# A recurrence taken by 1,024 tokens instead of 512, with its inputs in borrowed space, three spectrum buffers instead of four, and a new written order

## The chip, the core and the metric

The kernel runs on one core of a Trainium2 chip. A core has a matrix engine (TensorE, PE in the profile; PEld is its loading of weights), VectorE (DVE), ScalarE (ACT), GpSimd (POOL) and SyncE (SP), which here issues all transfers. SBUF is the working memory of 128 partitions; PSUM, in eight banks of 512 fp32 columns per partition, takes what TensorE computes; VectorE and ScalarE read it out. The metric is the device time of one execution in microseconds.

## The reference

A gated recurrence over 6,272 tokens feeds a long convolution with two multiplicative gates. Four batches, 256 channels, all fp32.

```python
sig = 1.0 / (1.0 + np.exp(-f_logit))
f = lower_bound + (1.0 - lower_bound) * sig
for t in range(S):
    h = f[:, t] * h + (1.0 - f[:, t]) * x[:, t]
    y[:, t] = h
proj = y @ w_proj                       # 256 -> 768: x1, x2, x3
X2 = np.fft.rfft(x2, n=S, axis=1)
H = np.fft.rfft(filter_fft, n=S, axis=0)
x2_conv = np.fft.irfft(X2 * H, n=S, axis=1)
out = (x1 * x2_conv * x3) @ w_out
```

## The kernel before

*Recurrence, `hgrn(b)`, lines 322 to 384.* The 6,272 tokens of a batch are 12 pieces of 512 and one of 128. For each piece two transfers bring the logits and x (L334), ScalarE applies the sigmoid of the negated logit (L337), GpSimd multiplies it into x (L339), and for each half of the channels (`kh`) TensorE transposes both (the step `su`, L351) into two PSUM banks, logits and products in the halves of each; ScalarE or VectorE makes the factor f from the transposed sigmoid (step `f`, L364 and L366), and VectorE runs the scan (L372), which starts from the last column of the scan before it and writes h to `HA`. The first 3,072 tokens are also copied behind the end (step `wrap`, L380), so that circular reads need no wrap. Inputs lie in three pairs of buffers (`XT`, `FL`), in batch 0 also in `gx`.

*Spectrum.* The convolution is a Fourier transform of length 49 x 128 in two factors. Step `P` (L725) projects h to x2, gathered by residues of 49, and its eviction writes `X2`, one row of `PW` = 116 half-words per channel pair, with gaps at columns 49 to 63 and 113 to 115 that hold zeros. `F1` (L737) and `F2` (L795) are the two transform factors, for 16 units of 8 channel pairs; F1 is evicted into one of four slots of `A`. The product with the filter's spectrum (L816 on VectorE straight out of PSUM, or an eviction by ScalarE and L825 on GpSimd) reads a buffer of `Hu`, 512 KB, loaded from DRAM (L772) for each unit; batches go through the units up and down in turn, so that the last buffers' units are still there for the next batch. `I2` (L835) and its eviction `Th` lead back. Four products per batch for the lone frequency columns (`mini`, `zm` at L761) read `Hm`, which lies in the gaps of `X2`.

*Gates and output.* `x13` (L400) projects h to x1 and x3, whose product is `zt` (evictions at L291, L293, L296, L298; products at L422 on VectorE or L431 on GpSimd, through `gx`). Step `I1` (L869) finishes the inverse transform, `y` (L875) multiplies it with `zt`, `proj` (L887) applies w_out, and an eviction and a store (L911) write the rows out.

*Preparation.* The filter's spectrum is computed on the core first (L637, L661, L679) and stored to DRAM; `afs` are the two buffers between its two factors, one of them the fourth spectrum buffer `Hx`.

*The order.* Nothing is scheduled by the compiler. Each step is recorded with what it reads and writes and with a cost per engine; the string `ORDER` then lists all steps in three characters each: number, engine and PSUM bank. Each engine, SP's queue of transfers too, takes its steps in that order, and semaphores follow from the reads and writes. The recurrence of batch b + 1 stands inside the spectrum and output steps of batch b; the first P of a batch needs all scans of it. `prod` marked MUL is L816, otherwise an eviction and a `pm` (L825).

Of the kernel before, what the change touches and what calls it, by code (L numbers as in the profile page):

```python
# [32 lines left out]
NH = 4  # L33
# [31 lines left out]
class Plan:  # L65
# [63 lines left out]
    "AAYA+gBBgAMYABIAZVACIBFgAaSBMgAtRBPgAmXAqSBTgAdTBIgA9YANIAcSBagAbUAoQAvVAwXA/WBCABDQBAGBGSBEIBogAOABdgBQAAPIBNQBWg"  # L129
    "BhgBHCBkgDwgBUVBOADxgBJYD8gBRTBVFEIgAuRArQBKQBSLBbWD9gBLABeYASIAQAATYADgAxTBXIAVYBcGAsVAyRBfTAUIEJgBYQBgDBpYBiWARI"  # L130
    "EUgBZABlIAWYBqSBmUBjGBrKApTBnMAhQAgQAfXAeTEVgAkRBuQDyABwSB1UBxKBvAB3WB2MBzSByYB4GDzYB+QD+AB0KCAWB6UCBGB/IEKAD0SB7M"
    "B5YAEYD4QD1CCFWD/YEggD5ICHUAFgD2KCGGEhgCIECDWCKUD6ICEGEASCCYELYCLEEBKEEWAlRECKEtgEFGCOQEsgCXUCPACJYAXYEGOCVSEWAEMQ"
    "CYMEiAEQWEXYCQUE4gEROCWCB8gAIACRME5gAKAESOCTSENABsYEYUCUCEOIEcWFCgCeSEdGCSYCZYEZMFDgCgQEjYAHAEeOCfCChACaSEaMEuACnQ"
    "EkWCbCEvYCoIClUElOE6AEoQCjSEmOFNgCmEFMgCkCCiYAjUCpYEpIEwUEnYAJAE7YCwWEqIExEETgE0SCxGEyMFWgCqQE1CCNgC1WCrAFXgE2KE8U"
    "FEAE/QC2OC3SFggFAAFFYE9MCuWFhgC4CAGgFBICvGAiTCMgFOACzWE+MFGSCyYC0GFPYFJQFHKC+UFqgFKAFIKFrgC6WC/EB9gC7GFQUAYYFLIDAS"
    "FYADHWFRMFTQDBCC5YFZYFSMDIGF1gDFSFUACsgDQWF0gDGCDDUFVID7gFiADKSDCYEzYEfgDEMFaQDRGEPYDLCDXWDJYCtgFbIErYDVUALADOSFjY"
    "DYODWEFcIDPCFdWDNgFsADTUD3gFeOFkQDUEMTgDSYFtYFfODgSFlAFnUEbgDhCFmICcgDeWFoEAnSDaSDZYF2AFpMDfGFuQF3YDbCDlWE3YFvIDnU"
    "EDYDmGDdgF+gDjSFwIDiYDoEEHgBtYFxWCdgDkCDpYJQVMfgFyODqQDcgJSFFzOC8gJRTDrAJVVMUgJWSC9gJTrJXFF4WF7QJYCJUYDuUF8IF5GF9I"
    "F/gDsgJZYJaTDvEF6ODtgJbQGAWDMgJdIMVAJcLGQUGigGBOJeYGGQGRMGUSGHAG0gGSWGVCMggGCUGTGGIRG9gGDEGEWGJJMhAGMUGFGGKRGNMGrg"
    "GOWGLJGWTGPGJfRGXDJgWJkQJiOJlXJhBJmIGeSJjYGYVGfCJnvJpUJqQJoYGZFJrMGaSJuRJsIGbCGjWJwJJtYGcUGnuJvQGdEJzSJ0RJxoGoYJ1C"  # L140
    "J4XGluJyYJ2BGsUGgSG1QJ3YGwEGhKGmYHQgJ5WJ6PG5AMrgHGSGtYMsgGkYJ9VJ7uGxYHHCJ+RGusJ8YGpWJ/FHMSGqGG3oGvYG+UG6YHZgKABHIW"
    "HNKG4YGyQHJGHAsHKSGzAG2YHigKBYG7WHLCHCsHBYKCQG/YG8GHORHRTHDYHrgHPJKDVHTDHVrHSYKHXKEAHUYKITKJHKFtKMSHWYMtAHEQKKrKGY"
    "KOKHaWKLYHFAMuYH+gH0UHcuHXSH1EH4QHeuHdYHYCHjUHbYHkYH5AHlsHfYIHgH2WMWYHgSH3GHnsHmYHsQHhCH6WHuoHoYIQgHpUHtYH7GMiYH/S"
    "HwoHvYHqEH8WKNQIBCIIUH9OHxYIZgIDqIRRICYIKEHyWITBKPoIEYKRUHzGIMsKQYKSTIiQIAYKTEIsgILYIFWIjAINYKUrKWVKVYKXTIGGKYNMXQ"
    "KZDIJYIVpI1gISYIaWIUYMYAMbUIeGMZIIWYIOSM3gMcEM4gKbXIPCMdMKaYI+gIXQKdHImSIYAIcuIbYMegMjUIfYInCIkQMkMIdYIoWIlAKcTMlM"
    "KgSMaYJHgIpGItQKerKiCIqUMnWIvoKfYIxAKhTNDgMoGIyYIgRIrMNEgIwYM5AMpOKlQI2UIhBKjrMvWIuYKnAI3YI6sKkYMzSM6YMwGKmQNPgI4E"
    "MxOKqRI7YNQgM0CIzUKsBM1KM7WI5YI0ENFAKrVKooKvTKttKpYM8GM/QNGYKuYKxDJIUM9ONbgNAAI8SNcgJMENBIKwXJKEK0WI9CJLYI/UKyvK2G"
    "K1RJBsKzYNHSK3BNRAK5WJDsJCYJAYK4YNLQNICNlgK7OJEYJFUNMANSYNmgNJKK6WJGEK+XNdANNINKgK/VNTTLAHJJYNeYK8uNXQNUDLBtK9YLDX"
    "NvgNYANVLLEWLCYMygLFHLISNwgLJVLKCNOgLNXJNYLGuLLFNfSNZILHYLPHNiUNgCLOWN6gNnANhKLMYN5gJOQNWgNjENoYLQuRtSJPANkMRuXLRY"
    "RvCLSQRwHLXSLTINxANpUMmYNsWLYKNqENyYLUQODgNtGOEgNrMLZSLVANuOLcULaCLWgNzQLdMRyWN0ALhSR0GN1IN2UN7ALmWONgN3ELiKOOgLeQ"  # L150
    "N8YLbgOFAM+gN4MLjSMqgLfALnOLrULkCOGYN9QLsMOAWN+ALoSOXgOBGN/IOYgM2gOHULpCNagOCOLwQOPAOKSLxILtWUwgOLCOQYLlgOIEOMKLyQ"
    "LuGOJML1SLzAORWL2KL0gRzROSGLqgL6UOZANCAOTOOUSOaYR1BU8gL7MU9gObWL3QOcGOVCOdOOWKOeUL4AL8WVJgVIgOfMUxgMEQL9GOgMLvgL/S"
    "MFIL5gOxUUyALggMAKOvQOyEL+gOhWOwIU+AOtUOiGO3QOuEOnWO4AOjTOoGO1ROkLUzYOpWO2BOrUOqGOzSU/YOsEOlQO0KVKAMBUOmAVLYMJWMCE"
    "O5SMKOO9QO6CMDgMGUO+IMOSMHEPDWMPKO7QPFuRxYR3SMIgO8AO/UPHuR4TR2YPGYPAEMLQR5KPtgR6DPBUPLWMMAPCMPbSPNuPEYPIYPTUR7YPdC"
    "R8QPXEPPuPOYPJRR+APMYPlVPKBPYYPVsPQYP2gR9QSBXMNgPmFPRRR/oPWYSDHPjVSAYPfqPSBPcYP/gSCQPUYPeYSGXPkFSHUSEoPgYPnSSIPSFY"
    "SJEPpQPoCPZWSKYQIgPqIPuUPaGPhSPysPrQP3WPiCPsIPzYSLVPwsP5GP4YQRQPvYSNFP6YQJSQSAP7uPxYQbgQAVSMUQEFSQRQNKP8YP0WSOsSSB"
    "QkgSRTSPYP1GQCtQBYSVQQFYSWUSXAQTWSTrQDYP9QSYsQUGSUYSaVSZYQLqQtgQOYQVTScFQGWP+AQWLQMYSbSQHGQcQQKYQ2gSdCQXUQgoQPWSeY"
    "QYESfTQeoQhYQQGQZRQlUShDQaJQfYRJgQ3WQnsQpEQmYQ/QQdYQ5GQiSQqYQ7GRAIQoYQuUQjCU0WQysQwERBQQvYU1GRSgQxYU4SQzYRCAU2OQrU"
    "VUgVVgU5CVAQQsEQ6YU6KRbgQ0WVBARDUQ1GU7gSgTVCISkSREEQ8YRKWSirSlRSmCRMuSjYSpQSnBRFUSrASqTSoYROuRNYRGESuSVEQSsrQ4YRPY"
    "SwCRHVVggSvXRINVFAStYVhgRTTRLYSxHVGIQ9VVWASyYSzSRVLS0XVHgQ+FVMQVXYRkgRXrS1CRQVVNAS2vRYYS4TRRFS5UVOIS3YS9XS6DRWYRcV"  # L160
    "S/HS7sVQSReFRgtS8YVYQVsgVRCVtgS+XRUYVZARfYVSKRhYTCWViARZUTAvVTgTDTRaETHSVaITBYVjYTIXTEGVcUTJCTFrRlQV4gVdETKvTGYTMW"
    "V5gRpARnoTNTTLYRmYTOGRdYTRXRqYTSSTTHTPrRoYVkQVuAVeMTQYRiWVlAVvYTWTTUqRjGTXUVmITVYTbVTYDVoWTdFTcRWCgVpOTZEWDgVwSV6A"
    "TaYVqORrUVxCTgQV7YTepRsEV0WVyKTfYTiAThRWMgV1GTlUVfgTmVTjpVrgTnEMQSU3YV2OToFTkYWNgTqUMRCTrRTpYTsETvSTtpV8UTuYTwKT0Q"
    "V9EV/WWEAT1IWWgTxSWXgWAGWFYVPgV+MT2QTyCWBOTzgT5UT3AMSgWGSVnYWOAT6MT+WWJQWHCWPYT/OT7UWggWKAT4gWhgWIKUAWT8EVzYWLIWQU"
# [32 lines left out]
def kernel(  # L197
# [780 lines left out]
```

## Time and profile before

| | us |
|---|---|
| median of 3 runs (460.45 to 461.36) | 460.54 |
| the profiled execution | 459.27 |
| its span, first to last instruction | 457.5 |
| TensorE busy | 443.7 |
| VectorE busy | 408.9 |
| ScalarE busy | 399.3 |
| GpSimd busy | 300.9 |

The granted clock of TensorE was 0.998 of full speed. "Busy" is a union in time; a group's "busy" is the sum of its instructions, which can overlap a little. Rows of groups read: line, engine, operation, output<-inputs, shapes, count | busy us, mean ns of one | idle us of the engine before them and what ended it. A row of a stage gives its length and then, for PE, PEld, DVE, ACT and POOL, busy us (instructions), the granted clock, the share of the 16 DMA engines and GB/s.

### The profile page before, as it was taken

The numbers are of one execution on the slowest core, as the hardware profiler recorded it, in microseconds if no ns is written. First come the engines' busy times: TensorE is split into PE (matmuls) and PEld (weight loads), VectorE is DVE, ScalarE is ACT, GpSimd is POOL, SyncE is SP. The second block draws the span as 40 slices with busy tenths as digits, with TensorE's granted clock in tenths as the row PEclk, the third lists the DMA queues.
The fourth block names the chain that finished last, engine by engine and source line by source line (L and its number), as shares of the span: only waits on it lengthen the run. The fifth ranks groups of instructions, "written<-read, shape, count | busy, mean of one in ns | idle before, by whom it ended". The sixth has DMA issues, their size and how long they took to land.

```text
span 457.5 us, 14613 instructions
## 1 busy us (share of the span) xinstructions
PE 443.7 (97%) x6009; PEld 346.2 (76%) x6009; DVE 408.9 (89%) x461; ACT 399.3 (87%) x550; POOL 300.9 (66%) x274
## 2 busy tenths in 40 slices
PE   8998999999999999999999999999999999999995
PEld 6876777767766889777668889767768897677784
DVE  7599996799999993999999986999999977999873
ACT  5989998889999989989998979999989868988563
POOL 4489892289899425778996616989896405976400
PEclk9999999999999999999999999999999999999999
DMA  8999999776979997477779995487969930575176
GB/s 323 407 366 333 357 356 347 284 262 203 313 259 298 326 339 299 179 250 246 241 272 287 350 315 240 142 288 297 308 205 308 351 124 18 192 238 179 48 294 271
DMA packets 46451, 122.59 MB, mean 268 GB/s; under 512 B 4528, under 2 KB 9648, under 8 KB 46384
## 3 DMA queue, kind: packets, MB, share of 16 engines
q1 hardware_dynamic: 46384, 121.65, 75.4%
q8 instruction: 47, 0.77, 0.7%
q14 instruction: 20, 0.16, 0.1%
HBM read 86.12 MB, written 31.98 MB: 258 GB/s over the span
## 4 chain that ended last, share of the span: by engine, by line
PE 70%; DVE 15%; ACT 8%; issue 4%; POOL 2%; DVEq 0%; ACTq 0%; POOLq 0%
PE PS L400 15%; PE PS L725 9%; PE PS L835 8%; PE PS L887 8%; PE PS L351 7%; DVE HA L372 6%; PE PS L737 6%; PE PS L795 6%; DVE ys L875 4%; PE PS L637 3%; PE PS L869 3%; PE PS L661 3%; ACT fTs L364 2%; ACT HA L291 2%; PE PS L603 2%
## 5 line engine op out<-in xcount | busy, mean ns | idle before, releaser
L339 POOL TENSOR_TENSOR XT<-XT,FL 128x1024 f32<-128x1024 f32 (+1 forms) x49 | 110.0, 2247 | 52.1 <-ACT FL L337 28.9
L372 DVE TENSOR_TENSOR_SCAN HA<-fTs,HA,PS 128x512 f16<-128x512 f32 (+1 forms) x96 | 113.2, 1203 | 1.1 <-ACT fTs L364 0.2
L400 PE MATMUL PS<-HA,W 128*128 128x490 f16 (+1 forms) x416 | 102.7, 367 | 1.0 <-DVE HA L372 0.4
L825 POOL TENSOR_TENSOR PP<-HA,Hu 98x1008 f16<-98x1008 f16 x38 | 79.7, 2104 | 5.1 <-ACT HA L291 2.7
L291 ACT CAST HA<-PS 128x1024 f16<-128x1024 f32 (+1 forms) x96 | 78.2, 837 | 5.3 <-PE PS L737 2.9
L431 POOL TENSOR_TENSOR zt<-gx 128x490 f16<-128x490 f32 (+1 forms) x43 | 52.1, 1217 | 45.0 <-DVE ys L875 16.7
L816 DVE TENSOR_TENSOR PP<-PS,Hu 98x1008 f16<-98x1008 f32 x58 | 68.1, 1200 | 0.0
L875 DVE TENSOR_TENSOR ys<-PS,zt 128x1024 fp32r<-128x1024 f32 (+1 forms) x52 | 58.9, 1152 | 7.8 <-PE PS L869 4.7
L887 PE MATMUL PS<-Wo,ys 128*128 128x256 f32 x392 | 58.2, 294 | 1.6 <-DVE ys L875 1.5
L364 ACT ACTIVATE fTs<-PS,cc 128x512 f32<-128x512 f32 (+1 forms) x83 | 54.8, 675 | 5.1 <-PE PS L351 4.3
L400 PEld LDWEIGHTS <-W 128*128 128x128 f16 x416 | 34.6, 97 | 30.4 <-issue 6.8
L835 PEld LDWEIGHTS <-PP 98*128 98x128 f16 x1024 | 49.9, 97 | 9.7 <-issue 1.6
L835 PE MATMUL PS<-VV,PP 98*128 98x98 f16 x1024 | 55.9, 206 | 0.3
L887 PEld LDWEIGHTS PS<-Wo,ys 128*128 128x128 f32 x392 | 49.7, 188 | 6.6 <-DVE ys L875 2.9
L291 ACT CAST Th<-PS 128x784 f16<-128x784 f32 x59 | 48.3, 821 | 6.6 <-PE PS L835 4.6
L293 ACT ACTIVATE gx<-PS 128x490 f32<-128x490 f32 (+1 forms) x84 | 48.3, 584 | 2.5 <-PE PS L400 1.5
L337 ACT ACTIVATE FL<-FL 128x1024 f32<-128x1024 f32 (+1 forms) x49 | 49.4, 1010 | 0.0
L725 PE MATMUL PS<-W,HA 128*128 128x256 f16 x392 | 44.6, 273 | 0.2
L351 PEld LDWEIGHTS PS<-iden,FL 64*128 64x128 f32 x736 | 31.2, 138 | 16.8 <-DVE HA L372 2.9
L725 PEld LDWEIGHTS <-HA 128*128 128x128 f16 x392 | 42.9, 142 | 1.3 <-DVE HA L372 0.3
L351 PE MATMUL PS<-iden,FL 64*128 64x64 f32 x736 | 42.2, 231 | 1.6 <-DVE HA L372 0.8
L291 ACT CAST X<-PS 128x1024 f16<-128x1024 f32 (+1 forms) x31 | 32.6, 1092 | 10.3 <-PE PS L725 9.0
(130 smaller groups left out, 745.6 us busy)
## 6 DMA issues: line engine op xcount, KB each, us to landing
FL<-in_f_logit_dram SPq DMA_DIRECT2D x45, 512.0 KB, 5.5
XT<-in_x_dram SPq DMA_DIRECT2D x45, 512.0 KB, 6.4
Hu<-H SPq DMA_DIRECT2D x39, 512.0 KB, 4.8
out_dram<-osb SPq DMA_DIRECT2D x22, 512.0 KB, 4.6
out_dram<-PP SPq DMA_DIRECT2D x16, 512.0 KB, 5.3
Hx<-H SPq DMA_DIRECT2D x13, 512.0 KB, 4.4
out_dram<-HA SPq DMA_DIRECT2D x10, 512.0 KB, 5.5
X<-in_moe_filter_fft_dram SPq DMA_DIRECT2D x9, 512.0 KB, 7.2
```

The lines of the kernel that those rows point to most:

```text
L291: nc.scalar.copy(dst, src)
L339: op("u", {"POOL": 0.1 + 0.553 * nb}, lambda e, xt=xt, ft=ft: nc.gpsimd.tensor_tensor(xt, xt, ft, op=AOP.mult), r=[("ft", k)], w=[("xt", k)])
L351: nc.tensor.transpose(bank(pb)[:, at[p] + j:at[p] + hn:nb], src[ps, j, cols], iden[ps, ps])
L364: nc.scalar.activation(fT, sT, AF.Identity, scale=by, bias=1.0)
L372: nc.vector.tensor_tensor_scan(h, fT, bank(pb)[:, 512 - hn:512 + hn], init, op0=AOP.mult, op1=AOP.add),
L400: nc.tensor.matmul(PS[:, p, 0:n], W13[:, kh, js], HA[:, HB[kh] + t0:HB[kh] + t0 + n], start=(kh == 0), stop=(kh == 1))
L725: nc.tensor.matmul(pp[:, r - r0, :], column(HB[kh], q_of(r)), W2[:, kh, :], start=(kh == 0), stop=(kh == 1))
L816: nc.vector.tensor_tensor(pr, px.unsqueeze(1).broadcast_to([TB, 2, UE, 63]), hh, op=AOP.mult)
L825: nc.gpsimd.tensor_tensor(pr, spec[:, o, :, 1:64].unsqueeze(1).broadcast_to([TB, 2, UE, 63]), hh, op=AOP.mult)
L835: nc.tensor.matmul(PS[:, ib + o, pr * TB:(pr + 1) * TB], PP[:TB, k, o, n, 2 * pr:2 * pr + 2, :], v[:TB], start=(n == 0), stop=(n == 1))
L875: nc.vector.tensor_tensor(late["ys"][:, yk, :, 0:rn * 128], PS[:, cb:cb + 2, 0:rn * 128], late["zt"][:].rearrange("p k r m -> p k (r m)") ...
L887: nc.tensor.matmul(po[:, i, :], late["ys"][:, yk, kh, i * 128:(i + 1) * 128], Wo[:, kh, :], start=(kh == 0), stop=(kh == 1))
```

## The change

From batch 1 on the recurrence takes six pieces of 1,024 tokens and the last of 128. A piece's transfers stay at 512 KB (two for the logits, two for x, each half of a partition's 8 rows), and so do sigmoid and multiplication. Logits and products are now transposed in steps of their own, each into two whole banks, with every eighth column written by one transpose; a gate and a scan take 1,024 columns. Batch 0 keeps pieces of 512 (function `single`), with the same buffers as before.

Inputs of one piece fill `XF` (which is `XT` and `FL` together); two further pieces land in `X2` (blocks of 2,048 half-words) and in what is left of `XF`; the second gate buffer `FT1` is block 6 of `X2`. So those loads wait until F1 of the batch before has read the block, and after the last scan the gaps of X2 are set to zero again (step `pad`, function `blank`). `Hm` therefore leaves the gaps for a tile of its own, in which the channel pair is the innermost index. There are three spectrum buffers, and `Hx` is gone: `afs` has two own tiles. `ORDER` is new throughout.

```diff
-NH = 4
+NH = 3
-    Hm = xv[:, :, Q:Q + 8].rearrange("m i (e a k) -> m e a k i", e=2, a=2)
-    Hu = konst.tile([128, NH - 1, 2, 2, UE * 64], F16, name="Hu")
-    Hx = konst.tile([128, 2, UE, 64], F32R, name="Hx")
+    Hu = konst.tile([128, NH, 2, 2, UE * 64], F16, name="Hu")
...
+    def load(b, t0, rows, dst, src, t):
+        n = 128 * rows
+        for j in range(0, rows, 4):
+            nj = min(4, rows - j)
+            op("load", {"SP": 0.46}, lambda e, j=j, nj=nj: nc.sync.dma_start(
+                dst(j // 4)[:, 0:nj], src[b, t0:t0 + n, :].rearrange("(p j) d -> p j d", p=128)[:, j:j + nj]),
+               w=[t[j // 4]], dma=0.38 * nj, lag=2.4, margin=MARGIN)
...
+    def scan(t0, n, kh, fT, tags, u, hn, src):
+        t1 = HB[kh] + t0
+        init = 0.0 if t0 == 0 else HA[:, t1 - 1:t1]
+        op("scan", {"DVE": 0.12 + 2.08 * n / 1000.0}, lambda e, pb: nc.vector.tensor_tensor_scan(
+            HA[:, t1:t1 + n], fT, u(pb), init, op0=AOP.mult, op1=AOP.add),
+           r=tags + ([("hn", kh, hn[0] - 1)] if t0 else []), w=[("hn", kh, i) for i in hn], src=src)
...
+    FT0 = fTs[:].rearrange("p a t -> p (a t)"), [("fT", 0), ("fT", 1)]
+    FT1 = X2[:, 2048 * 6:2048 * 7].bitcast(F32), [("xb", 6)]
...
+        slots = [(xf(0, 1), xf(2, 3)), (xb(0, 1), xb(2, 3)), (xb(4, 5), xf(4, 5))]
+        if b % 2 == 0:
+            slots = [slots[0], slots[2], slots[1]]
+        for p in range(S // 1024):
+            (ft, tf), (xt, tx) = slots[p % 3]
+            t0, nb = 1024 * p, 8
+            gate_in(b, t0, nb, ft, xt, tf, tx)
             for kh in range(2):
                 cols = slice(kh * 128, kh * 128 + 128)
+                def turn(e, pb, src, cols=cols):
+                    for j in range(nb):
+                        for q in range(2):
+                            ps = slice(64 * q, 64 * q + 64)
+                            nc.tensor.transpose(PS[:, pb + q, j::nb], src(j // 4)[ps, j % 4, cols], iden[ps, ps])
+                fT, tag = (FT0, FT1)[kh]
+                sf = op("su", {"PE": 0.5}, lambda e, pb, turn=turn, ft=ft: turn(e, pb, ft),
+                        r=tf + ["iden"], w=["qT"], take=2)
+                op("f", {"ACT": 0.145 + 1024 / 1200.0, "DVE": 0.11 + 1024 / 960.0},
+                   lambda e, pb, fT=fT, kh=kh: gate_f(e, fT, bank(pb), kh),
+                   r=["om"], w=tag, src=sf)
+                sv = op("su", {"PE": 0.5}, lambda e, pb, turn=turn, xt=xt: turn(e, pb, xt),
+                        r=tx + ["iden"], w=["qU"], take=2)
+                scan(t0, 1024, kh, fT, tag, bank, [2 * p, 2 * p + 1], sv)
+        (ft, tf), (xt, tx) = xf(0), xf(2)
+        single(b, NCHK - 1, ft, xt, tf, tx, [], [FT0, FT1])
+        op("pad", {"POOL": 2.0}, blank, w=[("xb", i) for i in range(7)] + ["pads"])
+
+    def blank(e):
+        nc.gpsimd.memset(xv[:, :, Q:64], 0.0)
+        nc.gpsimd.memset(xv[:, :, 113:PW], 0.0)
...
-        afs = [tmp.tile([128, 2, UE, 64], F32R, name="afs"),
-               Hx]
+        afs = [tmp.tile([128, 2, UE, 64], F32R, name=f"afs{i}") for i in range(2)]
...
-        f1 = op("F1", {"PE": 0.056 * UE}, mm, r=[("x2", g) for g in range(NX2)] + ["D1"], take=2)
+        f1 = op("F1", {"PE": 0.056 * UE}, mm, r=[("x2", g) for g in range(NX2)] + ["D1", "pads"] + [("xb", i) for i in range(
+            u * UE * PW // 2048, min(6, ((u * UE + UE - 1) * PW + 127) // 2048) + 1)], take=2)
...
-            nc.vector.tensor_tensor(zp[:TB, q % 2], px, Hm[:TB, :, :, :, es], op=AOP.mult)
+            nc.vector.tensor_tensor(zp[:TB, q % 2], px, late["Hm"][:TB, :, :, :, es], op=AOP.mult)
...
+            late["Hm"] = cv.tile([128, 2, 2, 2, NEP], F16, name="Hm")
```

More of the change, by code (lines that the diff above doesn't have):

```diff
@@ L651, in tails @@
             nc.gpsimd.memset(X2[:, NEP * PW:], 0.0)
-        op("pad", {"POOL": 0.6}, tails, w=[("raw", i) for i in range(7)] + [("x2", 1)])
+        op("pad", {"POOL": 0.6}, tails, w=[("raw", i) for i in range(7)] + [("x2", 1), "pads"])
         mX = tmp.tile([128, 2, NEP], F32R, name="mX")
@@ L772, in spectrum_load @@
         op("H", {"SP": 0.46}, lambda e: nc.sync.dma_start(
[L773 removed]
+            Hu[:, h][:HP].rearrange("p a e k -> p a (e k)"), turned(H[u // 2][u % 2])),
            r=[("H", u, i) for i in range(2)],
[L775 to L776 removed]
+           w=[("Hu", h)] + ([("hs", h, a) for a in range(2)] if first else []),
            dma=1.5, lag=2.0, margin=MARGIN)
```

274 lines of the change are left out of this document (135 added, 139 removed).

## The prediction

> **What bounds the kernel now.** I read the page first, then the busy time by stage, then the chain that ended last. The page gives the span and the share of each engine:
>
> ```profile
> span 457.5 us, 14613 instructions
> PE 443.7 (97%) x6009; PEld 346.2 (76%) x6009; DVE 408.9 (89%) x461; ACT 399.3 (87%) x550; POOL 300.9 (66%) x274
> ```
>
> The average hides the stages, so I cut the span where the TensorE's work changes: preparation with recurrence 0, then for batches 0 to 2 a spectrum stage (from the first F1 to the first I1) and an output stage (first I1 to the next P).
>
> ```profile
> core 0: us, PE busy (x) PEld busy (x) DVE busy (x) ACT busy (x) POOL busy (x), PEclk, DMA share, GB/s
> 0.00:73.80 73.80, 69.72 (x731) 54.72 (x731) 63.70 (x98) 65.97 (x87) 52.63 (x74) 1.00 0.96 352
> 86.30:145.20 58.90, 57.30 (x842) 40.17 (x844) 57.63 (x65) 55.65 (x83) 52.37 (x43) 1.00 0.77 252
> 145.20:169.80 24.60, 23.83 (x422) 20.51 (x421) 24.30 (x24) 22.04 (x30) 12.07 (x7) 1.00 0.95 336
> 182.30:243.00 60.70, 60.59 (x884) 43.20 (x884) 58.58 (x65) 56.47 (x87) 50.78 (x43) 1.00 0.71 237
> 243.00:271.30 28.30, 27.53 (x452) 22.96 (x446) 27.98 (x27) 24.88 (x34) 14.31 (x9) 1.00 0.92 321
> 282.80:341.00 58.20, 57.94 (x826) 40.77 (x826) 57.04 (x63) 54.80 (x85) 53.59 (x48) 1.00 0.69 234
> 341.00:368.90 27.90, 27.42 (x490) 23.65 (x490) 27.59 (x28) 25.22 (x35) 14.36 (x10) 1.00 0.88 314
> ```
>
> The fourth figure group of a row is VectorE. In the six stages it is busy for 253.1 of 258.6 us, and in the three output stages for 79.87 of 80.80. TensorE shows 98% too, but its matmuls are pipelined and a busy TensorE is not one at its peak. The chain decides between them. In the first output stage it runs along VectorE, alternating the output product (L875) and the scan (L372); the last row, from a later stage, is for the transposes:
>
> ```profile
> 159.94 1.12 DVE ys L875
> 161.06 2.38 DVE HA L372 x2
> 163.43 1.11 DVE ys L875
> ...
> 330.47 0.99 PE PS L351 x32
> ```
>
> So while the recurrence of one batch runs inside the stages of another, VectorE sets the pace, and instructions taken from it should shorten those stages.
>
> **The change, part by part.** The prices, from the groups by shape:
>
> ```profile
> L372 DVE TENSOR_TENSOR_SCAN HA<-fTs,HA,PS 128x512 f16<-128x512 f32 x88 | 109.7, 1270 | 1.0 <-ACT fTs L364 0.2
> L875 DVE TENSOR_TENSOR ys<-PS,zt 128x1024 fp32r<-128x1024 f32 x48 | 57.2, 1213 | 6.3 <-PE PS L869 3.2 <-PE PS L887 1.3 <-ACT osb L293 1.2
> L364 ACT ACTIVATE fTs<-PS,cc 128x512 f32<-128x512 f32 x79 | 53.6, 691 | 3.9 <-PE PS L351 3.0 <-DVE HA L372 0.2
> L291 ACT CAST X<-PS 128x1024 f16<-128x1024 f32 x27 | 26.4, 1019 | 9.8 <-PE PS L725 8.7 <-DVE ys L875 1.1
> L366 DVE TENSOR_SCALAR fTs<-PS,cc 128x512 f32<-128x512 f32 x17 | 12.7, 744 | 1.1 <-PE PS L351 0.5 <-ACT gx L293 0.2
> L761 DVE TENSOR_TENSOR zp<-PS,X 98x256 f16<-98x256 f32 x16 | 9.5, 597 | 0.4 <-PE PS L753 0.2
> L372 DVE TENSOR_TENSOR_SCAN HA<-fTs,HA,PS 128x128 f16<-128x128 f32 x8 | 3.7, 470 | 0.1
> L645 POOL MEMSET X<- 128x1920 f16 x1 | 1.7, 1722 | 0.0
> L875 DVE TENSOR_TENSOR ys<-PS,zt 128x256 fp32r<-128x256 f32 x4 | 1.7, 422 | 1.5 <-PE PS L869 1.5
> L650 POOL MEMSET X<- 128x384 f16 x1 | 0.7, 682 | 0.0
> ```
>
> *Scans.* Batches 1 to 3 go from 26 scans each to 14: 36 fewer. A token costs (1270 - 470) / 384 = 2.083 ns, which stays; the fixed part goes. By duration it is 1270 - 512 x 2.083 = 203 ns. But the chain shows two scans in 2.38 us, 1.19 each, so an instruction overlaps the next by some 0.08, and 0.12 us is what one really frees. 36 x 0.12 = 4.3 us; the ends are 0 (if VectorE is not the limit) and 36 x 0.203 = 7.3.
>
> *What the new order gives back to VectorE.* Counting both written orders by stage, in the six stages above it does 37 instructions fewer; the scans are 36 of them. The rest (5 gates and one y fewer; more evictions of F1 and Th and more products taken over from ScalarE) nets one instruction fewer, but longer ones: +1.0 us by their rows.
>
> *Hm* leaves the gaps of X2, where its innermost step is 116 half-words, for a tile where it is 1. L761 takes 597 ns for 256 columns; L875 with the same 256 columns, contiguous, takes 422. If the step is the reason, that is 0.175 us each, 12 of the 16 in the six stages: 2.1 us; otherwise 0. I take 2.1, because nothing else in the two rows differs by as much. The Trainium skill, "SBUF — State Buffer", section Door 1: The DMA port swizzle, has SBUF read in 16-byte lines, at full rate only with two or more accesses to a line; by it 232-byte steps are slow and this term is 2.1, without it 0, and the sum below would end 2.1 us higher. No run here has yet shown the same product with a contiguous operand.
>
> *ScalarE.* A gate over 1,024 contiguous tokens should cost what the eviction of 1,024 costs, 1.02 us, against 2 x 0.691. ScalarE is busy 92% of the six stages (239.1 of 258.6), below VectorE; I count its relief as nothing of its own.
>
> *Transposes.* Their number stays; each now writes every eighth PSUM word instead of every fourth. Thirty-two take 0.99 us; 1,152 are affected, 36 us in all. Both steps are non-contiguous, so 0; were each 5% slower, +1.8.
>
> *Pads.* Three times a memset of X2's gaps, 1.72 us, and of the tails, under 0.68, on GpSimd after the last scan. The next F1 needs it, but the 11 to 13 us of P lie between on TensorE: 0, with cover of about 9 us. If GpSimd came to it late, the first F1 would wait by the excess. Multiplications of the next batch queue behind it on GpSimd by 2.4 us, at a time when its load is light (14.31 us of 28.30).
>
> *Inputs in X2.* Four of six pairs use X2, so their loads wait for F1 instead of the transposes of the batch's own earlier pieces; the buffer of the second gate lies in block 6 and waits for F1 of units 13 to 15. By count, each spectrum stage has 6 scans of 1,024, against 14, 12 and 12 of 512 before: next to nothing moves. 0, and +2 if the second half's first scan slips into an output stage (one scan of 2.3 us in one batch). On SP these loads stand between the spectrum loads, which is the next point.
>
> *Three spectrum buffers.* 55 loads instead of 52. What matters is the time each has. First to last F2 of batches 0, 1, 2; then the durations of a product on GpSimd; the landing of spectrum loads in the three spectrum stages; the landing of input loads in the first two output stages:
>
> ```profile
> L795 PE MATMUL PS<-HA,FT x128: 266/269/287, 89.0 to 133.2; 64*128 64x256 f16 x128
> ...
> L795 PE MATMUL PS<-HA,FT x128: 266/269/287, 184.4 to 231.1; 64*128 64x256 f16 x128
> ...
> L795 PE MATMUL PS<-HA,FT x128: 266/269/287, 286.5 to 330.2; 64*128 64x256 f16 x128
> ...
> L825 POOL TENSOR_TENSOR PP<-HA,Hu x12: 2097/2107/2116, 190.8 to 232.3; 98x1008 f16<-98x1008 f16 x12
> ...
> DMA to landing us min/median/max: 3.4/4.6/6.5
> DMA to landing us min/median/max: 3.5/4.4/5.9
> DMA to landing us min/median/max: 3.4/5.8/7.1
> ...
> DMA to landing us min/median/max: 5.3/6.2/7.3
> DMA to landing us min/median/max: 4.0/6.3/9.2
> ```
>
> Fifteen intervals in 44 to 47 us: a unit every 3.0. A buffer is used again after four units now (12 us), after three then (9.0). Less about 2.1 us while a product holds it and 0.4 for the issue, a load has 9.5 us now and 6.5 then. Now the worst landing (7.1) fits; then only the tail does not. The new order also places 32, 32 and 33 transfers of 512 KB into the spectrum stages instead of 28, 27 and 26, so the DMA share there should go from 0.77, 0.71, 0.69 to about 0.85 to 0.88, near the output stages, where landings take 6.2 and 6.3. So some loads come late by a few tenths, and a VectorE product waiting for one holds up the scans and evictions queued behind it on VectorE, and through them the PSUM banks that TensorE needs. I take +1.5 (about one load in ten late by 0.3); ends 0 and +10.
>
> *Order around P.* P is limited by TensorE; one output projection more (about 1.2 us) stands among batch 1's P steps, a few tenths less elsewhere: +0.5. Preparation: inputs flow at 0.96 of the DMA, the same bytes stand ahead of the last input load; 0, between -2 and +2.
>
> *Sum.* -4.3 + 1.0 - 2.1 + 1.5 + 0.5 = -3.4 us. The profiled span of 457.5 becomes 454.1; the run of the profile, 459.27, becomes 455.9. The median of the three runs, 460.54, is 1.27 above that run, so I forecast 460.54 - 3.4 = 457.1.
>
> **The rivals.**
>
> *Late spectra (slower).* One mechanism: the loads of Hu, in the spectrum stages, with three buffers. For it: 6.5 us of room against landings of 6.2 and 6.3 at the DMA share that these stages approach. Against it: 4.4 to 5.8 at the share of now. If landings go to 6.3 and the two products of a unit hold the buffer for 1.2 + 2.1, a round takes 3.3 + 0.4 + 6.3 = 10.0 us instead of 9.0, 0.33 a unit. Over half of the 64 units that is 10.7, where the sum had 1.5: 457.1 + 9.2 = 466.3. It decides once the waits pass 1.5 + 3.4 = 4.9 us. The Trainium skill, "DMA: Bandwidth & Descriptors", section Latency and other measured facts, has HBM answer in 0.2 us on average and in 2 us at high load; by that, an estimate, 1.8 us are added to 4.6, 6.4 in all, and the room is just used up. The trace agrees in direction, 4.4 to 4.6 against 6.2 to 6.3.
>
> *Coarse scans (slightly slower).* A scan of 2.3 us holds two PSUM banks, and no y can run meanwhile; in output stages TensorE would run out of banks for I1 and projections. For it: VectorE there has 0.3 us of slack to lose per stage. Against it: gates and scans hold banks separately now, for less time in all. If each of the 18 long scans in output stages cost 0.27: +4.8, giving 461.9.
>
> *No effect.* TensorE, not VectorE, is the true limit (its 98%). Its work is the same; the sum keeps only +0.5 and relief cancels it: 460.5.
>
> *More than forecast.* ScalarE's relief counts too and no load is late: the fixed part by duration, -7.3 + 1.0 - 2.1 + 0.5 = -7.9: 452.6.
>
> **How the numbers follow.** Forecast 0.45, more than it 0.07, no effect 0.08, coarse scans 0.12, late spectra 0.28. What a measurement can tell from no change is 0.2%, 0.9 us. Faster: 0.45 + 0.07 = 0.52; same 0.08; slower 0.12 + 0.28 = 0.40. The forecast's own range is 454 to 459.5. For eight in ten the range goes from 452.5, the best case, to 467, just past late spectra as priced; a worse one and a slow preparation lie outside.
>
> **What would show it.** Right: scans of 1,024 at about 2.34 us; L761's successor near 0.42; VectorE still at 98% in the output stages, and these about as long, the spectrum stages shorter by a microsecond or more. Late spectra: VectorE or GpSimd products released by a DMA into Hu, spectrum stages longer. Coarse scans: VectorE idle in output stages, waiting for I1 of TensorE. The prediction fails if the waits for Hu together pass 5 us, if the transposes' time per 32 grows from 0.99, or if the preparation stage moves by more than 2 us.

## The result and the profile after

The changed kernel takes 466.33 us (median of four, 465.77 to 467.03) against 460.95 for the kernel before: a ratio of 1.0105, 95% interval 1.0063 to 1.0148. Run again beside other kernels it gave 1.0121 (1.0098 to 1.0143). It is slower by about 5.5 us, where I had forecast 3.4 us faster.

Its executions lie between 465.0 and 467.6 us, and the profiles are of single ones: the first profile belongs to the run of 467.03 us, a second one to a run of 464.99. The profile of before belongs to a run of 459.27, also at the fast end of its kernel, so the second profile is the one to lay beside it. The page's opening lines, first profile and then second:

```profile
span 465.0 us, 14490 instructions
...
PE 446.8 (96%) x6009; PEld 345.1 (74%) x6009; DVE 405.7 (87%) x418; ACT 391.0 (84%) x516; POOL 312.9 (67%) x280
```

```profile
span 463.0 us, 14490 instructions
```

VectorE has 43 instructions fewer and is busy only 3.2 us less. The groups by shape (first profile; the first row has 15 of the 36 long scans) show that the scan and the short product became as cheap as forecast:

```profile
L340 DVE TENSOR_TENSOR_SCAN HA<-fTs,HA,PS 128x1024 f16<-128x1024 f32 x15 | 35.1, 2339 | 0.1
L415 PE MATMUL PS<-iden,XF 64*128 64x64 f32 x576 | 24.4, 226 | 1.2 <-DVE ys L920 0.6 <-POOL XF L326 0.3 <-ACT fTs L333 0.2
L333 ACT ACTIVATE fTs<-PS,cc 128x1024 f32<-128x1024 f32 x17 | 19.0, 1120 | 0.8 <-PE PS L415 0.8
L807 DVE TENSOR_TENSOR zp<-PS,Hm 98x256 f16<-98x256 f32 x16 | 6.7, 417 | 1.1 <-PE PS L799 1.1
L430 POOL MEMSET X<- 128x1920 f16 x3 | 5.1, 1703 | 7.5 <-DVE HA L340 7.5
```

A scan of 1,024 takes 2,339 ns where I had put 2.34 us, the product with the contiguous `Hm` 417 ns instead of 597. The long gate takes 1,120 ns, where I had put 1.02 us. So the stages have to tell where the time went. These are busy times by stage of the second profile: spectrum and output stage of batches 0, 1 and 2 in turn. Below them stand two rows of before, for batch 1, cut at the same steps (first I1 at 241.7, first P at 270.2 us; the prediction had cut there 1.3 us later).

```profile
87.60:145.30 57.70, 55.87 (x823) 38.98 (x824) 55.30 (x57) 52.24 (x73) 52.29 (x43) 1.00 0.86 295
145.30:171.60 26.30, 24.64 (x443) 21.09 (x442) 25.42 (x19) 22.83 (x27) 14.81 (x7) 1.00 0.81 281
185.30:245.10 59.80, 59.16 (x828) 40.92 (x826) 55.91 (x58) 54.60 (x78) 53.20 (x44) 1.00 0.77 267
245.10:274.10 29.00, 27.04 (x481) 22.82 (x480) 27.42 (x21) 24.15 (x30) 16.93 (x10) 1.00 0.73 251
286.50:346.00 59.50, 59.24 (x834) 41.50 (x836) 57.04 (x57) 55.05 (x79) 52.62 (x46) 1.00 0.81 270
346.00:374.20 28.20, 27.25 (x485) 23.24 (x485) 27.39 (x22) 23.63 (x28) 14.81 (x8) 1.00 0.70 253
```

```profile
182.30:241.70 59.40, 59.29 (x840) 41.91 (x838) 57.41 (x63) 56.06 (x86) 50.10 (x43) 1.00 0.70 235
241.70:270.20 28.50, 27.77 (x481) 23.39 (x481) 28.04 (x28) 25.25 (x35) 14.99 (x10) 1.00 0.92 320
```

In batch 1's spectrum stage VectorE is busy 1.5 us less than before (55.91 against 57.41) and the stage is 0.4 us longer. TensorE's busy time stays where it was, 59.16 of 59.80. The view that answers this was there before the change, and I had not read it far enough. Part 4 of before's page, and a stretch of its chain of waits in the spectrum stage of batch 2 (start, length, what):

```profile
PE 70%; DVE 15%; ACT 8%; issue 4%; POOL 2%; DVEq 0%; ACTq 0%; POOLq 0%
```

```profile
19 pieces in order of time: start us, us, what
299.79 0.62 PE PS L400 x3
300.41 0.64 PE PS L351 x16
301.06 0.11 PE PS L753 x4
301.17 0.44 PE PS L795 x8
...
310.84 0.41 PE PS L400 x2
311.25 0.76 PE PS L835 x16
```

All 19 pieces are TensorE's. In the prediction I had quoted the chain of one output stage, batch 0's, where it does run along VectorE, and drew the conclusion for both kinds of stage.

One stretch is not the whole, though. If the pieces of before's chain are added up stage by stage, TensorE has 46%, 83% and 87% of the spectrum stages of batches 0, 1 and 2 and VectorE 5% to 10%. In batch 0's a third (32%) is ScalarE's and 10% GpSimd's. Of the output stages VectorE has 58%, 14% and 56%: batch 1's is TensorE's (69%). These rows are from batch 0's spectrum stage and from batch 1's output stage:

```profile
113.52 0.86 ACT HA L291
114.39 0.04 issue
114.43 0.82 ACT Th L291
```

```profile
248.13 0.50 PE PS L351 x16
248.63 2.33 PE PS L887 x16
250.96 0.70 PE PS L351 x16
```

So by this chain VectorE sets the pace in no spectrum stage, and in two of the three output stages.

TensorE's own rows hold a second thing. This is the timeline of TensorE in before: start, modelled length, line.

```profile
91.74 0.61 PE L795 MATMUL PS<-HA,FT 64*128 64x256 f16 x8
92.19 0.28 PE L753 MATMUL PS<-HA,FT 64*128 64x32 f16 x4
92.29 0.62 PE L795 MATMUL PS<-HA,FT 64*128 64x256 f16 x8
92.84 0.59 PE L400 MATMUL PS<-HA,W 128*128 128x490 f16 x2
93.26 0.61 PE L737 MATMUL PS<-D,X 128*128 128x128 f16 x8
93.71 0.99 PE L400 MATMUL PS<-HA,W 128*128 128x490 f16 x4
...
95.29 0.61 PE L737 MATMUL PS<-D,X 128*128 128x128 f16 x8
95.83 0.61 PE L795 MATMUL PS<-HA,FT 64*128 64x256 f16 x8
```

From start to start, F2 (L795) followed by the small product L753 takes 0.45 us, but followed by x1/x3 (L400) 0.55; F1 (L737) followed by L400 takes 0.45, followed by F2 0.54. What differs is whether TensorE changes between matmuls over all 128 (or 98) rows and matmuls or transposes over 64 rows (`64*128`). Over all successive steps of before the medians are 0.447 us for F1 to x1/x3 and 0.543 for F1 to F2; 0.414 for x1/x3 to itself and 0.509 to F2; 0.714 for I2 to x1/x3 and 0.807 to F2. A change costs 0.095 us. The Trainium skill, "TensorEngine Tiling (Array Packing)", section Key Properties, says that a change of tiling mode drains TensorE. If these `64*128` matmuls count as such a mode, the trace agrees, with a pause of 0.095 us a time; that the pause is a drain no trace shows. Counted in the written orders, before changes 256 times and the changed kernel 290 times: 34 x 0.095 = 3.2 us of TensorE that my sum did not have.

With that, TensorE's time from the first P on can be split for any profile: its steps at the distance that they have without a change, the changes, and the rest, which is waiting. Changes beside the filler matmuls of L603 are not counted. The column "P starts" is the length of the preparation. All times are in us and worked out from the traces.

| kernel (one profile each) | P starts | steps | changes | waiting | span |
|---|---|---|---|---|---|
| before | 73.7 | 343.2 | 207: 19.7 | 20.9 | 457.5 |
| changed, first profile | 75.5 | 342.8 | 237: 22.5 | 24.1 | 465.0 |
| changed, second profile | 75.4 | 342.8 | 237: 22.5 | 22.2 | 463.0 |

By the second profile the 5.5 us are 2.8 for changes of row mode, 1.7 for the later P (0.8 of it two x1/x3 products that the new order puts ahead of P), 1.3 more waiting, less 0.4 of steps. VectorE's relief had to show as less waiting, and there is none.

By stage, cut at the same steps, the three spectrum stages together grew by 0.4 us, the three output stages by 2.6, the four P stages by 0.5 and what follows the last P by 0.3; with the 1.7 of the later P that is the whole 5.5. Of the 30 changes 14 fall into the spectrum stages, 7 into the output stages and 9 behind the last P.

One part stands apart from these, GpSimd. It is busy some 12 us longer than before, and in the second profile's chain it has 20% and 17% of the first two spectrum stages, where before it had 10% and 1%. No run below takes this work away again, so what it costs is not known. The experiments test the other parts.

### The profile page after: what moved, and what is told of

It is laid out like the page before. It is cut to its first block, busy times and chain, and to the rows that moved or that the text cites. A ratio compares the mean times of both kernels' runs of the same rounds, so it can differ in the third digit from the quotient of the medians.

```text
span 465.0 us, 14490 instructions
## 1 busy us (share of the span) xinstructions
PE 446.8 (96%) x6009; PEld 345.1 (74%) x6009; DVE 405.7 (87%) x418; ACT 391.0 (84%) x516; POOL 312.9 (67%) x280
## 4 chain that ended last, share of the span: by engine, by line
PE 47%; POOL 6%; issue 6%; DVE 5%; ACT 4%; DMA 3%; SPq 0%; DVEq 0%; ACTq 0%; POOLq 0%
PE PS L446 13%; PE PS L932 7%; PE PS L880 7%; PE PS L415 5%; PE PS L840 5%; PE PS L782 4%; PE PS L770 3%; PE PS L914 3%; POOL PP L870 2%; DMA X<-in_x_dram 2%; DVE HA L340 2%; DVE ys L920 2%; POOL XF L326 2%; DMA Hu<-H 1%; POOL X L326 1%
## 5 line engine op out<-in xcount | busy, mean ns | idle before, releaser
L861 DVE TENSOR_TENSOR PP<-PS,Hu 98x1008 f16<-98x1008 f32 x86 | 101.0, 1199 | 5.9 <-PE PS L840 1.9
L870 POOL TENSOR_TENSOR PP<-HA,Hu 98x1008 f16<-98x1008 f16 x42 | 88.2, 2108 | 8.4 <-ACT HA L280 4.4
L477 POOL TENSOR_TENSOR zt<-gx 128x490 f16<-128x490 f32 (+1 forms) x49 | 59.5, 1221 | 40.6 <-DVE ys L920 28.3
L280 ACT CAST HA<-PS 128x1024 f16<-128x1024 f32 (+1 forms) x88 | 72.7, 846 | 8.2 <-PE PS L782 4.4
L326 POOL TENSOR_TENSOR XF<-XF 128x1024 f32<-128x1024 f32 (+1 forms) x25 | 52.9, 2119 | 34.3 <-ACT XF L324 27.1
L340 DVE TENSOR_TENSOR_SCAN HA<-fTs,HA,PS 128x512 f16<-128x512 f32 (+2 forms) x42 | 64.7, 1556 | 0.8 <-ACT fTs L333 0.5
L840 PE MATMUL PS<-HA,FT 64*128 64x256 f16 x512 | 39.1, 271 | 0.7 <-ACT HA L280 0.3
L782 PEld LDWEIGHTS <-X 128*128 128x128 f16 x512 | 31.0, 98 | 8.5 <-issue 2.9
L782 PE MATMUL PS<-D,X 128*128 128x128 f16 x512 | 36.8, 219 | 0.3 <-ACT gx L282 0.2
L340 DVE TENSOR_TENSOR_SCAN HA<-X,HA,PS 128x1024 f16<-128x1024 f32 (+1 forms) x18 | 36.4, 2024 | 0.5 <-ACT X L333 0.2
```

The costliest lines, as they stand in the source:

```text
L280: nc.scalar.copy(dst, src)
L326: op("u", {"POOL": 0.1 + 0.553 * nj}, lambda e, j=j, nj=nj: nc.gpsimd.tensor_tensor(xt(j // 4)[:, 0:nj], xt(j // 4)[:, 0:nj], ft(j // 4)[: ...
L340: op("scan", {"DVE": 0.12 + 2.08 * n / 1000.0}, lambda e, pb: nc.vector.tensor_tensor_scan(HA[:, t1:t1 + n], fT, u(pb), init, op0=AOP.mult ...
L782: nc.tensor.matmul(pa[:, i, :], X2[:, j:j + 128], D1[:], start=True, stop=True)
L840: nc.tensor.matmul(PS[:, xb + e2, :].rearrange("p (i k) -> p i k", k=64)[:, :, ks], FT[rows, o, r, :], A[rows, ka:ka + UE, r, ks], start=( ...
L861: nc.vector.tensor_tensor(pr, px.unsqueeze(1).broadcast_to([TB, 2, UE, 63]), hh, op=AOP.mult)
```

## The experiments

*A fourth spectrum buffer.* `Hx` comes back as fourth buffer, in the space of one `afs`; the order stays. To make room, the lone columns (`zm`) read the weights `W13` in place of `Hm`, so their factors are left out of the result. It was run twice.

```diff
-NH = 3
+NH = 4
-afs = [tmp.tile([128, 2, UE, 64], F32R, name=f"afs{i}") for i in range(2)]
+afs = [tmp.tile([128, 2, UE, 64], F32R, name="afs"), Hx]
...
-nc.vector.tensor_tensor(zp[:TB, q % 2], px, late["Hm"][:TB, :, :, :, es], op=AOP.mult)
+nc.vector.tensor_tensor(zp[:TB, q % 2], px, W13[:TB].rearrange(...)[:, :, :, :, es], op=AOP.mult)
```

> The changed kernel with a fourth spectrum buffer again (it shares space with one of the two preparation buffers, as before), in the changed kernel's own written order; three loads are dropped (52 instead of 55) and each of the others stands where it stood, so each may start one unit earlier. To make room the product of the lone columns reads the first gate weights instead of Hm, so these columns of the output are left out; the time of that product is the same. Theory B (the three buffers cost the time: every step that reads a spectrum waits a little, and the pipeline of products behind it): 2.5 to 5 us below the changed kernel's 466.3, that is 461.3 to 463.8. Theory X (inputs in X2, later and in bursts, and long scans cost it): within 1 us of 466.3. Theory O (the new order is merely packed worse): within 1 us of 466.3, since the order stays.

> The changed kernel with four spectrum buffers, in its own order, once more: 464.3 us (ratio 1.0064 in the first run), so 2 to 2.6 us under the changed kernel's 1.0105 to 1.0121; 465.5 or more would put the fourth buffer's worth in doubt.

Measured: 464.31 us, ratio 1.0064 (1.0043 to 1.0085), and 464.55 us, 1.0086 (1.0068 to 1.0104). Against 1.0105 and 1.0121 for three buffers, taken in this order, the fourth is worth 0.41% and 0.35%, 1.6 to 1.9 us, each uncertain by 1.3 us or more. Its ten runs lie between 463.8 and 465.6, the ten of the changed kernel between 465.0 and 467.6. Both profiles of the changed kernel have a row in which a VectorE product waits for a spectrum load, first profile and second (waiter, what it waits for, us in all, times, longest):

```profile
DVE PP L861 <- DMA Hu<-H: 1.1, 1, 1.1
```

```profile
DVE PP L861 <- DMA Hu<-H: 0.7, 1, 0.7
```

In before and in the second profile with four buffers there is no such row. The first profile with four buffers has one that is just as long, at 98.2 us, where the fourth buffer is used for the first time:

```profile
DVE PP L864 <- DMA Hx<-H: 1.2, 1, 1.2
```

So spectra do come late with three buffers, but these rows do not explain the gain of the fourth. What it is worth is measured; by which wait it is lost is not shown. The rival had priced it at 10.7.

*Remade orders, first attempt.* The changed kernel, before, and before with three buffers each get another written order, in which steps, banks and engines were changed one at a time wherever a replay of the order with the traces' durations became shorter. The replay did not know of the changes of row mode.

```diff
-ORDER = (...)
+ORDER = (...)      # well over half of some 2,400 steps moved
```

> The changed kernel, all steps the same, in another written order (steps moved one at a time, banks exchanged, some evictions moved between ScalarE and VectorE). Theory O: with an order as well packed as any, the loss of 5.4 us goes: 461 or less, and it then lies within 1.5 us of the kernel before with an order made in the same way (sent with it). Theories B and X: it may gain from the new order, but stays 4 us or more above the kernel before treated in the same way.

> The kernel before, all steps the same, in another written order made in the same way as for the changed kernel. It is the control: if the order before had slack of its own, it gains as much as the changed kernel does. All theories: between 450 and 462; Theory O: the gain is at least 4 us smaller than that of the changed kernel; Theories B and X: the gains are alike within 2 us.

> The kernel before with only three of its four spectrum buffers in use (55 loads instead of 52), in an order made in the same way; pieces of 512 tokens, inputs and Hm as before. Theory B: 4 to 8 us above the kernel before in its remade order. Theories X and O: within 1.5 us of it.

Measured: 490.38, 479.38 and 483.81 us (ratios 1.0628, 1.0389, 1.0479). All are slower than the orders they came from, so no expectation of a gain by order held; these orders change row mode 324, 298 and 302 times, and their preparation alone is longer by 7 to 9 us. One difference can be read, three buffers against four, 4.4 us, but with a single order each it is not the buffer's alone.

*More changes of row mode in the kernel before.* Twenty-two pairs of neighbouring TensorE steps are exchanged, so that it changes 300 times instead of 256. As a control, TensorE's steps are exchanged at 18 places (22 moves in all) such that the count stays 256. One of the 22 places and one of the control:

```diff
-x13 x13 x13 x13 F2  mini F2 x13
+x13 x13 x13 F2  x13 mini F2 x13
...
-F1 x13 x13 F1  x13 F2 F1 x13
+F1 x13 x13 x13 F1  F2 F1 x13
```

> The kernel before, with 22 of TensorE's steps each moved a few places in the written order and nothing else changed. They are chosen so that TensorE goes back and forth more often between matmuls over all 128 rows (F1, x1/x3, I2, P, projection) and matmuls or transposes over 64 rows (transposes of the inputs, F2, mini, I1): 300 times instead of 256. Theory T (TensorE's queue is the path, and each such switch holds it for 0.095 us, as F1 to F1 0.444 us and F1 to F2 0.540 us in the trace of before): 44 x 0.095 = +4.2 us, 460.9 to 465.1. Theory V (VectorE sets the pace, as in the prediction): VectorE's work is the same, so within 0.5 us of before, 460.4 to 461.4. In between, some +2 us, if TensorE has slack in part of the stages.

> A control for the 22 exchanges in the kernel before that raised TensorE's switches to 300: here 18 pairs of neighbouring TensorE steps (and 4 steps past others) are exchanged as well, but always such that the number of switches stays 256. Theory T (a switch costs TensorE 0.095 us and TensorE is the path): within 0.7 us of before, 459.6 to 461.0. Theory D (any exchange disturbs an order in which everything fits closely, switches or not): about as slow as the other, 464 to 466.

Measured: 465.96 us, ratio 1.0121 (1.0100 to 1.0143), for the 44 further changes; 462.82 us, ratio 1.0043 (1.0024 to 1.0062), for the control. Exchanging steps costs 2.0 us in itself, which theory T did not expect. The 44 changes cost 0.78% beyond it (about 0.5% to 1.1%), 3.6 us or 0.08 each, against 4.2 forecast. The control has 18 exchanges on TensorE where the other has 22; if the cost of exchanging is scaled to 22, some 3.1 us are left, 0.07 each. The split agrees: waiting is about 23 us in both profiles, some 2 more than in before, and they differ by the changes. So a change of row mode is paid in full or nearly so by the end of the kernel, as far as one control can show it.

*Fewer changes in the changed kernel.* Thirteen steps are moved, 264 changes instead of 290. One place, in the last output stage:

```diff
-I1 proj proj I1   proj I1 I1 proj
+I1 proj proj proj I1   I1 I1 proj
```

> The changed kernel, with 13 of TensorE's steps each moved within the written order and nothing else changed, so that it switches 264 times between full-row and 64-row matmuls instead of 290. Theory T: 26 x 0.095 = -2.5 us, 466.3 to 463.8. Theory V: within 0.5 us of the changed kernel, 465.8 to 466.8.

Measured: 470.58 us, ratio 1.0217 (1.0191 to 1.0242), 4.4 us slower than the changed kernel. Both theories missed. The changes did become cheaper (211 from P on, 20.0 us against 22.5), but the waiting went from 22.2 to 30.0 us. The last output stage and batch 1's spectrum stage (59.80 us in the row above) carry most of it, here the last output stage of the changed kernel's second profile, and then both of this one:

```profile
436.80:463.00 26.20, 21.69 (x305) 18.75 (x304) 17.19 (x15) 11.59 (x12) 0.11 (x1) 0.98 0.67 266
```

```profile
184.90:246.60 61.70, 60.29 (x837) 42.23 (x834) 56.74 (x58) 54.82 (x78) 53.04 (x44) 1.00 0.77 262
439.60:468.30 28.70, 21.71 (x305) 18.82 (x304) 17.19 (x15) 11.59 (x12) 0.18 (x1) 0.99 0.61 243
```

Three projections in a row wait for a `y` of VectorE, where an I1 in between had filled the time. At this place the order changes row mode to cover a wait. These 13 moves did not make the changes cheaper to have; whether others would, this run can't say.

*Scans halved again.* The changed kernel, with each scan of 1,024 issued as two of 512.

```diff
+            for a in range(0, n, CH):
+                m = min(n, a + CH)
+                nc.vector.tensor_tensor_scan(HA[:, t1 + a:t1 + m], fT[:, a:m], u(pb)[:, a:m],
+                    init if a == 0 else HA[:, t1 + a - 1:t1 + a], op0=AOP.mult, op1=AOP.add)
```

> The changed kernel, in its own order, with each of the 36 scans over 1,024 tokens issued as two of 512 that follow each other, as before the change. Theory V (VectorE sets the pace): the whole gain of the scans is given back, 36 x 0.12 = +4.3 us, 470.6. Theory T: VectorE is idle for 59 us of the span and takes most of it there: 0 to +1.5 us, 466.3 to 467.8.

Measured: 474.43 us, ratio 1.0312 (1.0286 to 1.0339), 8.7 us over the changed kernel's 1.0121. More than theory V's 4.3, because the second half waits for the first's last column: a half starts 1.37 us after the one before it (median), not 1.19, so a pair costs 1.37 + 1.19 - 2.25 = 0.31 us more than a long scan. At that price theory V would have 36 x 0.31 = 11.2 us, and the measured 8.7 lies between the theories. The stages are what tells:

```profile
87.70:145.50 57.80, 56.62 (x822) 39.24 (x822) 55.72 (x62) 52.17 (x73) 52.70 (x43) 1.00 0.85 297
145.50:173.70 28.20, 25.82 (x443) 21.38 (x442) 26.78 (x26) 22.90 (x27) 14.41 (x7) 1.00 0.76 263
187.50:247.70 60.20, 59.21 (x830) 41.02 (x830) 56.27 (x63) 54.67 (x78) 53.08 (x44) 1.00 0.77 264
247.70:279.30 31.60, 28.00 (x482) 23.25 (x481) 29.33 (x28) 24.85 (x30) 17.22 (x11) 1.00 0.71 245
291.70:351.70 60.00, 59.41 (x832) 41.61 (x832) 57.04 (x62) 55.15 (x79) 52.74 (x46) 1.00 0.80 269
351.70:382.40 30.70, 28.20 (x485) 23.41 (x485) 29.41 (x29) 23.84 (x28) 14.86 (x8) 1.00 0.65 235
```

In the changed kernel 18 of the long scans stand in the three output stages and 18 in the three spectrum stages. The output stages grow from 83.5 to 90.5 us, 0.39 a scan; the spectrum stages from 177.0 to 178.0, 0.06 a scan. More work for VectorE is paid in the output stages, at more than its own price, and hardly in the spectrum stages.

*The short product alone.* Before, with `zm` reading the contiguous `W13` (the lone columns' factors are left out of the result).

```diff
-nc.vector.tensor_tensor(zp[:TB, q % 2], px, Hm[:TB, :, :, :, es], op=AOP.mult)
+nc.vector.tensor_tensor(zp[:TB, q % 2], px, W13[:TB].rearrange(...)[:, :, :, :, es], op=AOP.mult)
```

> The kernel before, with the lone columns' products (L761) reading a contiguous tile (the weights of x1 and x3) in place of Hm in the gaps of X2: these columns of the output are wrong, all else is done in the same order. Both theories expect 597 ns to become about 420 for each of 16. Theory V (VectorE sets the pace in the spectrum stages too, as the prediction had it): 16 x 0.175 = -2.8 us, 457.5. Theory S (in the spectrum stages TensorE sets the pace, and only in the output stages VectorE does): 0 to -0.7 us, 459.6 to 460.3, since these products lie in the spectrum stages alone.

```profile
L758 DVE TENSOR_TENSOR zp<-PS,W 98x256 f16<-98x256 f32 x16 | 6.7, 418 | 0.6 <-PE PS L750 0.6
```

Measured: 418 ns a product, as expected, and 459.99 us, ratio 0.9985 (0.9966 to 1.0005): -0.7 us, not to be told from nothing, and theory V's -2.8 lies outside. The three spectrum stages, 176.6 us before, take 175.9. This is the spectrum stages' half of the verdict, on the kernel before itself.

*Inputs in X2.* F1 reads `W13` in place of X2; loads into X2 wait for P's evictions alone.

```diff
-matmul(pa[:, i, :], X2[:, j:j + 128], D1[:], ...)
+matmul(pa[:, i, :], W13[:, i % 2, 128 * (i // 2):128 * (i // 2) + 128], D1[:], ...)
...
-r=[("x2", g) ...] + ["D1", "pads"] + [("xb", i) ...]
+r=[("x2", g) ...] + ["D1", "pads", "W13"]
```

> The changed kernel, in its own order, with F1 reading a constant tile (the weights of x1 and x3) in place of X2: the output is not the reference's, since P's result goes unused. The loads of inputs into X2 then wait for P's evictions only, no longer for F1, and on SP's queue nothing stands behind a wait for F1 (21.2 us in nine waits in the changed kernel). TensorE and all engines do the same work in the same order. Theory X (the landing of inputs in X2's space is what costs: late bursts of loads, and spectrum loads that stand behind them): 462.3 to 464.8. Theories T and B (switches of TensorE, three spectrum buffers): within 0.7 us of the changed kernel, 465.6 to 467.0.

Measured: 465.75 us, ratio 1.0112 (1.0087 to 1.0136), the changed kernel's own. No cost shows of where the inputs land. Theory X falls, though the smallest gain that it named, 1.5 us, lies at the edge of the interval.

*The changed kernel again, and the order of its preparation.*

```diff
-ORDER = (...)      # steps ahead of batch 0's P, as changed
+ORDER = (...)      # the same steps in the order and on the engines of before
```

> The changed kernel once more, unaltered, for a second profile and a narrower ratio: 465.2 to 466.9 us by every theory. What the two profiles of it differ by is what a comparison of single profiles can't tell.

> The changed kernel with the preparation (all steps ahead of batch 0's P) in the order and on the engines of the kernel before, as far as the steps are the same; from P on everything stands as it was. In all profiles of the changed kernel and its variants P starts at 75.4 to 75.5 us, in those of before at 73.7 to 74.1. If that is the written order of the preparation: -1.6 us, 464.7. If it is the work itself or the memory that the change lays out differently: within 0.5 us of the changed kernel.

> The changed kernel with four spectrum buffers (lone columns left out as in the first run with four) and the preparation in the order of the kernel before. Theory B (with three buffers, a small shift of time makes spectrum loads late; with four it doesn't): the microsecond that P starts earlier is kept, 1 us under the same kernel with its own preparation, 463.3 against 464.3. If the preparation's order is worth nothing, or the loss lay elsewhere: as slow as it or slower.

Measured: the changed kernel 467.04 us (1.0121); with before's preparation 467.15 us (1.0124, 1.0099 to 1.0149); with that and four buffers 464.33 us (1.0093, 1.0076 to 1.0111) against 464.55 without. P does start earlier, by 0.9 us with three buffers and 0.5 with four, and nothing of it is left at the end. With three buffers the profile, of the slowest of its five runs (467.99 us), has more products waiting for spectra:

```profile
DVE PP L858 <- DMA Hu<-H: 2.4, 3, 1.4
```

With four it has none, yet there too the medians differ by only 0.2 us, within the scatter, and the ratios not at all in its favour (1.0093 against 1.0086). So theory B's account of where the microsecond went isn't confirmed; why it is lost stays open.

*Orders remade with the changes counted.* The same for all four structures, with 0.095 us a change and the preparation left alone.

```diff
-ORDER = (...)
+ORDER = (...)      # over 1,000 of some 2,400 steps moved; about 90 evictions on another engine
```

> The kernel before with a remade order: from P of batch 0 on, steps, PSUM banks and the engine of evictions changed one at a time, kept where a replay of the order with the traces' durations gets shorter, each of TensorE's switches counted at 0.095 us. Switches 248 to 260. The first remade orders left the switches out and changed the preparation too, and came out at 479; this one should lie between 457 and 468. It is the base for the next three, made in the same way.

> The kernel before with three spectrum buffers in place of four, and an order remade in the same way. Theory B (three buffers cost, whatever the order): 3 to 6 us above the remade order of before. Theory O (the loss lies in the one written order): within 1.5 us of it.

> The changed kernel (three buffers, long scans) with an order remade in the same way. Theory B: 3 to 6 us above the remade order of before, as much as with three buffers in the kernel before, so that the long scans and the contiguous Hm bring nothing. Theory V (VectorE's relief counts): below before with three buffers by 4 us or more. Theory O: within 1.5 us of the remade order of before, or under it.

> The changed kernel with a fourth spectrum buffer (in the space of the filters' scratch, the lone columns' factors left out of the computation as in the first run with four buffers) and an order remade in the same way. Theory B: 3 to 6 us below the changed kernel's remade order, and within 1.5 us of before's. Theory V: 4 us or more under before's remade order. Theory O: within 1.5 us of all the others.

| remade order of | us | ratio | changes in all | P starts | changes from P on | waiting |
|---|---|---|---|---|---|---|
| before, four buffers | 465.01 | 1.0094 (1.0066 to 1.0121) | 250 | 73.7 | 19.3 | 27.0 |
| before, three buffers | 467.32 | 1.0139 (1.0106 to 1.0172) | 248 | 74.4 | 19.2 | 29.0 |
| changed, three buffers | 470.69 | 1.0219 (1.0188 to 1.0251) | 284 | 75.7 | 21.8 | 28.8 |
| changed, four buffers | 467.73 | 1.0150 (1.0123 to 1.0177) | 280 | 75.9 | 21.6 | 25.9 |

None beats the order it came from, so none is a better kernel. Made in one way, they hint at the structure's share, with one order each: the control above shows that exchanges alone can shift the time by 2.0 us. The fourth buffer is worth 2.3 us in before and 3.0 in the changed kernel (theory B had 3 to 6: right in kind, smaller in size). At equal buffers the changed kernel is 2.7 and 3.4 us slower, where theory V had it 4 faster; theory O, all within 1.5, falls too. The rows split it again: 2.3 and 2.6 us of changes, 2.2 and 1.3 of later P, and 1.1 and 0.2 us less waiting, which is all that VectorE's relief shows. The remade orders did start from the two written ones, so whether long scans need more changes of row mode by nature, or only inherited them, is not settled.

## Why the prediction was wrong

*The bound.* "So while the recurrence of one batch runs inside the stages of another, VectorE sets the pace" is the step that failed. In the spectrum stages it does not hold: a halved scan costs 0.06 us there, the products shortened by 2.8 us bring 0.7, and VectorE has 5% to 10% of the chain. These stages are two thirds of the six stages' time. In the output stages a halved scan costs 0.39 us, so there more work for VectorE is paid; but in before's chain even batch 1's output stage was TensorE's.

*The sum.* Scans, -4.3: half of them lie in spectrum stages, where the gain is next to nothing; in the output stages the new order used the room up, with one 1,024 piece's scan more (36 short ones' worth against 34), about 1 us more TensorE steps and 7 more changes. The three output stages went from 80.9 to 83.5 us, the spectrum stages from 176.6 to 177.0. Hm, -2.1: by duration right, 597 to 417 ns, by effect -0.7. (The Trainium skill, "SBUF — State Buffer", section Door 1: The DMA port swizzle, has strides beyond a 16-byte line slow; the two durations agree.) TensorE's work "is the same": its steps are, but 34 changes of row mode, 2.8 to 3.2 us, were not in it. This term was missing altogether, not mis-sized.

*Three buffers, +1.5.* Nearly right in size: 1.6 to 1.9 us by its own order, 2.3 and 3.0 by remade ones. The mechanism, loads that come late by a few tenths, is seen only in part: one product of the second profile waits, for 0.7 us.

*The terms at nothing.* Transposes (226 ns each against 223 to 231 before), the pads (the 7.5 us of idle time in their row is GpSimd waiting for the last scan), the inputs in X2 and ScalarE's relief: no run showed a cost or gain. Preparation: 0, between -2 and +2; P started 1.7 us later. Order around P, +0.5: the four P stages took 0.5 us more.

*The rivals.* That the time came out at 466.3, the very figure of late spectra, is chance, for it did not come by that mechanism: the products waited 0.7 to 1.1 us for `Hu`, not over 5. "TensorE, not VectorE, is the true limit" had the right engine for the spectrum stages of batches 1 and 2, at a chance of 0.08, and it too took TensorE's work as unchanged.

In all, of some 5.5 us: about 3 are changes of row mode (34 at 0.07 to 0.095; inferred, as removing 26 of them did not pay), and about 2 come back with the missing buffer (measured, by a way that is not shown). P starts 1.7 us late, but starting it earlier gained nothing. These parts were measured in different ways and overlap, GpSimd's added work has no price, and the rest stays open.

## What to carry over

Read the chain of waits in each kind of stage, not in the one where it shows what one hopes for; a share of 98% for two engines is decided there. In a matmul stream count the changes between 64-row and full-row work as instructions with a price, and compare them before and after a new order. A missing buffer can cost 2 us although a profile shows only about 1 us of waiting for it, so such a cost is settled by a run with the buffer and not by the rows of waits.

## What was not expected of the hardware

A change between full-row and 64-row matmuls holds TensorE for 0.095 us in every pair of steps listed above. A scan that begins with the last column of the scan just before it starts 1.37 us after it at 512 columns, against 1.19 for an independent one. And an order that fits closely is fragile: exchanges of TensorE steps at 18 places, with as many changes of row mode as before, cost 2.0 us (1.1 to 2.9).
